# A spectral filter and a state-space layer behind one gate: order of the first loads, folds three row groups ahead, and GpSimd in written order

## The chip, the cores and the metric

The kernel runs on one core of a Trainium2 chip. A core has TensorE (PE in the profile; its weight loads are PEld), VectorE (DVE), ScalarE (ACT), GpSimd (POOL) and SyncE (SP), each with its own instruction queue, and DMA engines that they share. The metric is device time in microseconds: 359.55 us is the median of three runs before the change (358.8, 359.55, 362.57). Inputs and the output are bf16.

## The reference

x has 2048 tokens of 1024 features. Two branches read it, and a gate per token mixes them:

```
g = sigmoid(sum(x * gate_w, over features))
a = irfft2(rfft2(x) * (w_r + i w_i))            # over tokens and features
Lam = Lambda_re + i Lambda_im;  Lam_bar = exp(exp(log_dt) * Lam)
Bu = x @ (((Lam_bar - 1) / Lam) * (B_re + i B_im)).T
h_t = Lam_bar * h_(t-1) + Bu_t                  # a scan over the 2048 tokens
b = 2 * Re(h @ (C_re + i C_im).T) + x * Dskip
out = g * a + (1 - g) * b
```

## The kernel before

**Tokens.** Row group j (0 to 15) is the 128 tokens that are j modulo 16. `load_x(j)` brings it transposed into `xQ[:, :, j, :]` (L194, a transposing DMA of 256 KB from SP).

**The spectral front** is one pass over the 16 row groups. `fold(j)` (L645 to L650) adds and subtracts the two halves of the features on DVE and leaves `preT`. `fd(j)` (L330) multiplies by the constant G on PE (eight matmuls, L334), and ACT copies the product to X1 (L337). `s1(j)` (L340) is the first step of the transform over tokens (four matmuls with the constant T2, L346); A1 is copied out by ACT or, for row groups 6, 8, 10, 12, 14 and 15, by DVE (L349). GpSimd issues its store to DRAM (L350, 256 KB). A1 lies in the tiles `CT`, eight row groups in each half; the transposes of C into the same tiles (`load_C`, L547) come later, when the stores have read them. `keep_A1` (L353) keeps one column of A1.

`front()` (L739) issues for its row group j: the fold of j + 2, `fd(j + 1)`, `s1(j)`, and then some pieces of the tables.

**The tables** (`make_tab`, L207) are the rotations of the state-space scan: four tables of two blocks. Each goes through DVE (angles, L212, L774, L776), ACT (L778 Abs, L779 sine, L781 cosine, L223, L228), DVE (L229, L234), and GpSimd: it spreads `rz` (L214, L215) and casts sine and cosine to bf16 (L219, L225). The buffers of sine and cosine are single, so the sine of one table waits for the casts of the table before. A table is a generator of four pieces; `front` runs one piece in row groups 4 to 7, and two in each from 8 on.

A group of small DVE operations (L786 to L815), which waits for the sine and cosine of a few angles on ACT, stands in DVE's order between row groups 2 and 3.

**The state-space branch.** `unit(c, q)` projects 256 tokens by half of B (64 matmuls, L298; two copies by ACT, L300), and DVE turns, scans (L273) and turns back. The first unit begins in row groups 14 and 15. `early` multiplies by C (L562). These are woven with the later spectral steps until 300 us; then come the last tiles and the output.

**The gate** (`gate`, L673) is 32 matmuls; then GpSimd stores z to DRAM (L681) and loads it back in another order as `zt` (L683).

**W's columns** (`load_Wcols`, L709): two GpSimd copies give `Wp` and `Wf` a value everywhere (they read row group 12 of xQ, L710 and L711), ten GpSimd DMAs fetch two columns of w_r and w_i (L716 to L720, small packets), and three GpSimd copies make `Wc` (L722 to L724). PE reads it at L382, DVE at L389.

**What sets the order.** PE, DVE and ACT run in the order in which the program is written (`manual_schedule`, L167). For GpSimd and SP a planner chooses the order when the program is built. In the profile GpSimd spread all of `rz` first (16 to 22 us), issued three stores of A1 (22 to 26), waited for row group 12 of x (36.5), and went through W's columns, with two stores among them, to 51.9; casts and stores followed.

SP issued x, T2 and B in the order of L661 to L665: the list gives the row groups behind each of which one load of B follows (5, 7, 9 and 11 to 15). G's two loads were issued by ACT at the very start (L174), ahead of five small vectors (L177).

Of the kernel before, what the change touches and what calls it, by code (L numbers as in the profile page):

```python
# [14 lines left out]
BF16 = mybir.dt.bfloat16  # L15
# [8 lines left out]
P = 128  # L24
# [85 lines left out]
def kernel(  # L110
# [17 lines left out]
    nc = tc.nc  # L128
# [4 lines left out]
    cG = nc.inline_tensor(hc["G"], name="c_G").ap()  # L133
# [30 lines left out]
    gta = ictx.enter_context(tc.tile_pool(name="gta", bufs=2, side="right"))  # L164
    psA = ctx.enter_context(tc.tile_pool(name="psA", bufs=2, space=PSUM, reuse_waits="tile"))
    psU = ctx.enter_context(tc.tile_pool(name="psU", bufs=2, space=PSUM, reuse_waits="tile"))
    guard = tc.manual_schedule(engines={mybir.EngineType.PE, mybir.EngineType.DVE, mybir.EngineType.Activation})  # L167
    guard.__enter__()


    fft = {}
    fft["G"] = pre.tile([P, 2, 4, K], BF16, name="G_sb")
    for cls in range(2):
        nc.scalar.dma_start(out=fft["G"][:, cls], in_=cG[:, cls])  # L174
    vec8 = tmp.tile([8, 5, P], BF16, name="vec8")
    for i, src in enumerate((B_Lambda_re, B_Lambda_im, B_log_dt, B_Dskip, gate_w)):
        nc.scalar.dma_start(out=vec8[:, i, :], in_=src.rearrange("(j p) -> j p", p=P))  # L177
# [15 lines left out]
    def load_x(j):  # L193
        nc.sync.dma_start_transpose(out=xQ[:, :, j, :], in_=x_v[j])  # L194

    def load_T2(a, b):
        nc.sync.dma_start(out=fft["T2"][:, a:b], in_=cT2[:, a:b])
# [3 lines left out]
    def load_B(n):  # L201
        for _ in range(n):
            jb, ri = next(parts_B)
            nc.sync.dma_start_transpose(out=BT[jb][:, ri], in_=(B_B_re, B_B_im)[ri][P * jb:P * (jb + 1), :])  # L204


    def make_tab(jp):  # L207
        sh = [P, 2, TC]
        js = slice(2 * jp, 2 * jp + 2)
        ang = tmp.tile(sh, FP32, name="ang")  # L210
        for j in range(2):
            nc.vector.tensor_scalar_mul(out=ang[:, j], in0=tau_f, scalar1=thp[:, 2 * jp + j:2 * jp + j + 1])  # L212
            jb = 2 * jp + j
            nc.gpsimd.tensor_copy(out=rz[:, jb, :], in_=r_sb[:, jb:jb + 1].to_broadcast([P, TC]))  # L214
            nc.gpsimd.memset(rz[:, jb, 0:1], 0.0)  # L215
        sn_f = tmp.tile(sh, FP32, name="sn_f")
        cs_f = tmp.tile(sh, FP32, name="cs_f")
        yield from sincos(tmp, ang, sh, sn_f, cs_f, "rot")
        nc.gpsimd.tensor_copy(out=tab[:, 1, js, :], in_=sn_f)  # L219
        t1 = tmp.tile(sh, FP32, name="t1")  # L220
        t2 = tmp.tile(sh, FP32, name="t2")
        for j in range(2):
            nc.scalar.activation(out=t1[:, j], in_=sn_f[:, j], func=ACT.Copy, scale=ci[:, 2 * jp + j:2 * jp + j + 1])  # L223
        yield
        nc.gpsimd.tensor_copy(out=tab[:, 0, js, :], in_=cs_f)  # L225
        for j in range(2):
            jb = 2 * jp + j
            nc.scalar.activation(out=t2[:, j], in_=cs_f[:, j], func=ACT.Copy, scale=ci[:, jb:jb + 1])  # L228
            nc.vector.scalar_tensor_tensor(out=tab[:, 2, jb, :], in0=cs_f[:, j], scalar=cr[:, jb:jb + 1], in1=t1[:, j],  # L229
                                           op0=ALU.mult, op1=ALU.subtract)  # L230
        yield
        for j in range(2):
            jb = 2 * jp + j
            nc.vector.scalar_tensor_tensor(out=tab[:, 3, jb, :], in0=sn_f[:, j], scalar=cr[:, jb:jb + 1], in1=t2[:, j],  # L234
                                           op0=ALU.mult, op1=ALU.add)
# [73 lines left out]
    def vector(us):  # L309
        owed[0] += us  # L310
        while work and owed[0] > 0:
            cost, piece = work.pop(0)
            piece()
            owed[0] -= cost
        if not work:
            owed[0] = min(owed[0], 0.0)
# [221 lines left out]
    def step():  # L538
        v = next(gen, None)
        while v in ("ia", "ib"):  # L540
            (after_ia if v == "ia" else after_ib)()
            v = next(gen, None)
        return v
# [99 lines left out]
    preTs = {}  # L643

    def fold(j):  # L645
        preTs[j] = gta.tile([P, 8, P], BF16, name="preT", bufs=3)
        to = preTs[j].rearrange("p d (g q) -> p d g q", g=2)
        lo, hi = (xQ[:, 4 * i:4 * (i + 1), j, :].rearrange("p d (q g) -> p d g q", g=2) for i in range(2))
        nc.vector.tensor_add(out=to[:, 0:4], in0=lo, in1=hi)  # L649
        nc.vector.tensor_sub(out=to[:, 4:8], in0=lo, in1=hi)  # L650
# [4 lines left out]
    def keep_warm(n):  # L655
        psw = psA.tile([P, 2, K], FP32, name="psw", tag="ps")
        for i in range(n):
            nc.tensor.matmul(psw[:, i % 2, :], lhsT=idle[:, 0:P], rhs=idle, start=True, stop=True)

    keep_warm(8)  # L660
    for j, b in enumerate((0, 0, 0, 0, 0, 1, 0, 1, 0, 1, 0, 1, 1, 1, 1, 1)):  # L661
        load_x(j)
        if j in (1, 2, 6):
            load_T2(*{1: (0, 2), 2: (2, 8), 6: (8, 16)}[j])
        load_B(b)  # L665
    assert step() == "front"
    fold(0)
    fft["fd"](0)
    fold(1)
    zsb = tmp.tile([P, K], FP32, name="zsb")  # L670
    zt = cpool.tile([P, 16], FP32, name="zt")

    def gate():  # L673
        zps = psA.tile([P, K], FP32, name="zps_g", tag="ps")
        for d8 in range(8):
            for i in range(4):
                nc.tensor.matmul(zps[32 * i:32 * (i + 1), :], lhsT=gw32[:, d8, :], rhs=xQ[:, d8, 4 * i:4 * (i + 1), :],
                                 start=(d8 == 0), stop=(d8 == 7), tile_position=(0, 32 * i))
        nc.scalar.copy(out=zsb.rearrange("p (m j) -> p m j", j=4), in_=zps.rearrange("p (j m) -> p m j", j=4))
        with nc.allow_non_contiguous_dma(reason="gate by token tiles"):  # L680
            nc.gpsimd.dma_start(out=z_dram.rearrange("(n i j) -> i n j", i=4, j=4),  # L681
                                in_=zsb[0:P:32, :].rearrange("i (n j) -> i n j", j=4))
            nc.gpsimd.dma_start(out=zt, in_=z_dram.rearrange("(t p) -> p t", p=P))  # L683
# [25 lines left out]
    def load_Wcols():  # L709
        nc.gpsimd.tensor_copy(out=Wp.rearrange("p r b c -> p (r b c)"), in_=xQ[:, 0, 12, 0:64])  # L710
        nc.gpsimd.tensor_copy(out=Wf, in_=xQ[:, 0, 12, 0:2])  # L711
        with nc.allow_non_contiguous_dma(reason="two columns of W"):
            for ri, W in enumerate((A_w_r, A_w_i)):
                fl = W.rearrange("s k -> (s k)")[K:K + (S - 1) * (K + 1)].rearrange("(s k) -> s k", k=K + 1)
                at = lambda b: bass.AP(W.tensor, W.offset + K + (K + 1) * b, [[16 * (K + 1), P], [K + 1, 15], [1, 2]])
                nc.gpsimd.dma_start(out=Wp[:, ri, 0:15], in_=at(0))  # L716
                nc.gpsimd.dma_start(out=Wp[0:P - 16, ri, 15], in_=fl[15:16 * (P - 16):16, 0:2])
                nc.gpsimd.dma_start(out=Wp[P - 16:P - 1, ri, 15], in_=fl[16 * (P - 16) + 15:S - 1:16, 0:2])
                nc.gpsimd.dma_start(out=Wp[P - 1:P, ri, 15:16, 0:1], in_=W[S - 1:S, K:K + 1].unsqueeze(0))
                nc.gpsimd.dma_start(out=Wf[:, ri:ri + 1], in_=W.rearrange("(p b) k -> p b k", b=16)[:, 0, 0:1])  # L720
        Wc = fft["Wc"].rearrange("p b (c r) -> p r b c", r=2)
        nc.gpsimd.tensor_copy(out=Wc[:, :, :, 1], in_=Wp[:, :, :, 0])  # L722
        nc.gpsimd.tensor_copy(out=Wc[:, :, 1:16, 0], in_=Wp[:, :, 0:15, 1])
        nc.gpsimd.tensor_copy(out=Wc[:, :, 0, 0], in_=Wf)  # L724

    def chain(*items):
        for item in items:
            yield from item

    def halves(gen, n):  # L730
        for _ in range(n):
            next(gen, None)
# [4 lines left out]
    tables = iter(())  # L737

    def front(pieces=0):  # L739
        j = at[0]  # L740
        at[0] += 1
        if j + 2 < 16:
            fold(j + 2)
        if j + 1 < 16:
            fft["fd"](j + 1)
        fft["s1"](j)
        for _ in range(pieces):
            next(tables, None)
# [41 lines left out]
    for _ in sincos(sp, ang2, [P, 2, 8], s2c, c2c, "a2"):  # L790
        front()
# [25 lines left out]
    tables = chain(*(make_tab(jp) for jp in range(4)))  # L817
    while at[0] < 16:
        j = at[0]
        front(0 if j < 4 else 1 if j < 8 else 2)  # L820
        if j == 8:
            fft["keep_A1"](0)
        if j == 12:
            load_Wcols()
        if j >= 14:
            halves(ssm, 1)
            vector(2.0)
    gate()
    fft["keep_A1"](1)
    load_small()  # L830
    load_B(8)
    for _ in tables:
        pass
    tctx.close()
    for q in range(8):
        load_C(q)
# [95 lines left out]
```

## Time and profile before

| what | us |
|---|---|
| median of the runs | 359.55 |
| the profiled execution | 363.51 |
| its span, first to last instruction | 361.7 |
| PE busy | 328.7 (91%) |
| DVE busy | 295.2 (82%) |
| ACT busy | 156.8 (43%) |
| GpSimd busy | 45.8 (13%) |

| stretch, us | what runs in it | PE busy | DVE busy | ACT busy | DMA share | GB/s |
|---|---|---|---|---|---|---|
| 0 to 10 | first loads | 3.57 | 0.33 | 0.00 | 0.94 | 156 |
| 10 to 24 | row groups 0 to 3 | 12.83 | 9.00 | 9.07 | 1.03 | 222 |
| 24 to 48 | row groups 4 to 9 | 18.13 | 18.21 | 14.21 | 1.20 | 179 |
| 48 to 58 | row groups 9 to 11 | 1.35 | 2.03 | 5.52 | 1.17 | 265 |
| 58 to 77 | the last row groups, three tables | 14.22 | 13.18 | 10.58 | 1.07 | 228 |
| 77 to 87 | first unit, gate | 10.00 | 4.94 | 3.85 | 0.95 | 231 |
| 87 to 151 | units, first outputs | 62.32 | 61.94 | 16.52 | 0.55 | 108 |
| 151 to 300 | units, outputs, spectral steps | 148.13 | 136.07 | 76.93 | 0.65 | 170 |
| 300 to 361.7 | last tiles | 58.14 | 49.49 | 20.10 | 0.77 | 133 |

How to read it: the slices of the page divide the span in 40, each digit the busy share in tenths; PEclk is the granted clock of TensorE in the same way. The chain of waits goes back from the last instruction to what released it. The timeline gives start, duration, engine, line, operation, output and inputs, and in brackets the idle time before it with what ended it. Waits are inferred from semaphores, so the name in a bracket can be the wrong one of several. A DMA share can read above 1 in a short stretch.

### The profile page before, as it was taken

The page shows a single profiled execution, that of the slowest core. Times are in us where ns is not written, and L with a number is a line of the kernel's source. Part 1 is how long each engine was busy: PE and PEld are TensorE (multiplying, and loading weights), DVE is VectorE, ACT ScalarE, POOL GpSimd, SP SyncE. Part 2 cuts the span into 40 slices and gives each one's busy share as a digit, 9 for nine tenths or more (in the row PEclk, how much of TensorE's full clock was granted, in tenths as well). Part 3 has the DMA queues.
Part 4 walks back from the last instruction along what each step waited for, and adds up shares of the span by engine and source line. Part 5 has one row for each costly group of instructions (what it writes and reads, how often), then busy time and mean ns, then how long its engine had stood idle before and what let it go on. Part 6 is the DMA issues. An engine that isn't in the chain of part 4 may idle for free.

```text
span 361.7 us, 5961 instructions
## 1 busy us (share of the span) xinstructions
PE 328.7 (91%) x2314; PEld 205.1 (57%) x2314; DVE 295.2 (82%) x443; ACT 156.8 (43%) x200; POOL 45.8 (13%) x80
## 2 busy tenths in 40 slices
PE   3778826599999998999999999999999999999996
PEld 1222211147898647465666657577975786555652
DVE  0567818656999999999999999999995499999961
ACT  0494725572332312365565656245663334344410
POOL 1270853222100000000000000000000001212220
PEclk9698985879999999999999999999999999999999
DMA  9999999996999123178899996297622106975794
GB/s 158 214 201 227 169 197 295 197 193 204 121 197 208 26 87 90 43 201 177 231 291 247 284 241 178 80 248 195 175 63 87 58 2 104 136 139 119 115 134 159
DMA packets 96252, 58.69 MB, mean 162 GB/s; under 512 B 71096, under 2 KB 86976, under 8 KB 96096
## 3 DMA queue, kind: packets, MB, share of 16 engines
q1 hardware_dynamic: 91408, 50.40, 62.0%
q0 software_dynamic: 4448, 6.86, 11.9%
q10 hardware_dynamic: 368, 1.06, 1.2%
q8 instruction: 18, 0.29, 0.4%
q14 instruction: 10, 0.08, 0.1%
HBM read 26.30 MB, written 17.83 MB: 122 GB/s over the span
## 4 chain that ended last, share of the span: by engine, by line
PE 60%; DVE 21%; SPq 8%; DMA 5%; ACT 2%; issue 2%; POOL 1%; DVEq 0%; ACTq 0%; POOLq 0%
PE ps_y L562 22%; PE psu L298 19%; DVE h L273 6%; SPq L194 6%; PE ps_h L562 4%; PE ps_id L593 3%; SPq L204 2%; PE ps_is L501 2%; PE ps_is L476 2%; PE ps_is L477 2%; DMA Wp<-in_A_w_r_dram 2%; PE ps_s L452 2%; DVE su L260 2%; DVE h L261 2%; DMA Wp<-in_A_w_i_dram 2%
## 5 line engine op out<-in xcount | busy, mean ns | idle before, releaser
L298 PE MATMUL psu<-xQ,BT 128*128 128x256 bf16 x1024 | 115.2, 273 | 0.8 <-ACT ye L580 0.5
L298 PEld LDWEIGHTS <-BT 128*128 128x128 bf16 x1024 | 99.4, 98 | 15.5 <-issue 2.4
L562 PE MATMUL ps_y<-CT,h 128*128 128x512 bf16 x448 | 101.3, 379 | 0.0
L562 PEld LDWEIGHTS <-h 128*128 128x128 bf16 x512 | 49.6, 98 | 55.2
L273 DVE TENSOR_TENSOR_SCAN h<-rz,h 128x1024 bf16<-128x1024 f32 x32 | 72.0, 2280 | 0.4
L300 ACT CAST h<-psu 128x1024 bf16<-128x1024 f32 x32 | 32.4, 1012 | 70.5 <-PE psu L298 70.5
L334 PE MATMUL ps_fd<-G_sb,preT 128*128 128x512 bf16 x128 | 37.4, 445 | 19.7 <-DVE preT L649 13.5
L608 POOL DMA_DIRECT2D BT<-y_scratch x10 | 11.9, 1187 | 240.7 <-DVE BT L602 236.5
L334 PEld LDWEIGHTS <-preT 128*128 128x128 bf16 x128 | 12.6, 109 | 43.3 <-DVE preT L649 25.5
L580 ACT ACTIVATE ye<-ps_y,omg 128x512 f32<-128x512 f32 x20 | 12.7, 684 | 35.1 <-PE ps_y L566 30.6
L260 DVE TENSOR_TENSOR su<-h,tab 128x2048 bf16<-128x2048 bf16 x16 | 19.6, 1223 | 4.3 <-ACT h L300 3.5
L454 ACT CAST X<-ps_s 128x1024 bf16<-128x1024 f32 x16 | 16.2, 1014 | 10.9 <-PE ps_s L452 10.9
L261 DVE TENSOR_TENSOR h<-h,tab 128x2048 bf16<-128x2048 bf16 x16 | 19.6, 1225 | 0.8
L285 DVE TENSOR_TENSOR h<-h,tab 128x2048 bf16<-128x2048 bf16 x16 | 19.6, 1225 | 0.5
L337 ACT CAST X<-ps_fd 128x1024 bf16<-128x1024 f32 x16 | 16.1, 1006 | 8.1 <-PE ps_fd L334 8.1
L284 DVE TENSOR_TENSOR sg<-h,tab 128x2048 bf16<-128x2048 bf16 x16 | 19.5, 1219 | 0.0
L649 DVE TENSOR_TENSOR preT<-xQ 128x512 bf16<-128x512 bf16 x16 | 11.1, 695 | 9.0 <-DMA xQ<-in_A_x_dram 9.0
L479 ACT CAST C<-ps_is 128x1024 bf16<-128x1024 f32 x16 | 16.1, 1007 | 3.5 <-issue 3.5
L503 ACT CAST ZT<-ps_is 128x1024 bf16<-128x1024 f32 x16 | 15.5, 1021 | 4.3 <-PE ps_is L501 4.3
L229 DVE SCALAR_TENSOR_TENSOR tab<-cs_f,cr,t 128x256 bf16<-128x256 f32 x8 | 4.8, 642 | 14.7 <-ACT t L223 14.7
L346 PE MATMUL ps_s<-X,raw 64*128 64x512 bf16 x64 | 11.1, 428 | 5.7 <-ACT X L337 5.7
L593 PE MATMUL ps_id<-raw,ZT 128*128 128x256 bf16 x128 | 15.9, 273 | 0.0
(182 smaller groups left out, 364.9 us busy)
## 6 DMA issues: line engine op xcount, KB each, us to landing
y_scratch<-ye SPq DMA_DIRECT2D x20, 256.0 KB, 3.5
turn_scratch<-CT POOLq DMA_DIRECT2D x16, 256.0 KB, 4.7
Bb<-turn_scratch SPq DMA_DIRECT2D x16, 256.0 KB, 4.6
turn_scratch<-C SPq DMA_DIRECT2D x16, 256.0 KB, 5.4
raw<-turn_scratch SPq DMA_DIRECT2D x16, 256.0 KB, 4.3
Wb<-in_A_w_r_dram SPq DMA_DIRECT2D x32, 127.8 KB, 4.0
Wb<-in_A_w_i_dram SPq DMA_DIRECT2D x32, 127.8 KB, 4.1
out_dram<-BT SPq DMA_DIRECT2D x14, 256.0 KB, 3.2
```

What stands on the lines that cost most here:

```text
L194: nc.sync.dma_start_transpose(out=xQ[:, :, j, :], in_=x_v[j])
L260: nc.vector.tensor_mul(out=su, in0=u[:, ::-1], in1=bc(1))
L261: nc.vector.tensor_mul(out=u, in0=u, in1=bc(0))
L273: nc.vector.tensor_tensor_scan(out=seg, data0=rz[:, js].rearrange("p j t -> p (j t)"), data1=seg, initial=0.0, op0=ALU.mult, op1=ALU.add)
L284: nc.vector.tensor_mul(out=sg, in0=u[:, ::-1], in1=bc(3))
L285: nc.vector.tensor_mul(out=u, in0=u, in1=bc(2))
L298: nc.tensor.matmul(psu[:, j, :], lhsT=BT[4 * q + j][:, ri, d8, :], rhs=xQ[:, d8, :, 16 * c:16 * (c + 1)], start=(d8 == 0), stop=(d8 == 7))
L300: nc.scalar.copy(out=u[:, ri].rearrange("p b (m j) -> p b m j", j=16), in_=psu.rearrange("p b (j m) -> p b m j", j=16))
L334: nc.tensor.matmul(ps[:, cls, :], lhsT=preTs[j][:, 4 * cls + d4, :], rhs=G_sb[:, cls, d4, :], start=(d4 == 0), stop=(d4 == 3))
L454: nc.scalar.copy(out=X2, in_=ps2)
L562: nc.tensor.matmul(psy, lhsT=hs[c, jb // 4][:, ri, jb % 4, P * tq:P * (tq + 1)], rhs=CT[ri][:, jb, 512 * dh:512 * (dh + 1)], start=(i == 0 ...
L593: nc.tensor.matmul(pse[:, slot, :], lhsT=ZT_t[:, i, tb, :], rhs=fft["Gi"][:, i, :], start=(kb == 0), stop=(kb == 1))
```

## The change

Five edits. G's loads move from ACT's queue to SP's, behind row group 0 of x. No load of B stands among the first eight row groups; one follows each of row groups 8 to 15. Folds run three row groups ahead, with a fourth `preT` buffer. GpSimd runs in written order: a store of A1 stands behind its row group, and the table's spreads and casts where the pieces stand. `load_Wcols` moves from behind row group 12 to behind the gate, the last copy of A1's column and the small constants; the second eight loads of B, and the call that drains the tables, move ahead of the gate.

```diff
-    guard = tc.manual_schedule(engines={mybir.EngineType.PE, mybir.EngineType.DVE, mybir.EngineType.Activation})
+    guard = tc.manual_schedule(engines={mybir.EngineType.PE, mybir.EngineType.DVE, mybir.EngineType.Activation, mybir.EngineType.Pool})
...
     fft["G"] = pre.tile([P, 2, 4, K], BF16, name="G_sb")
-    for cls in range(2):
-        nc.scalar.dma_start(out=fft["G"][:, cls], in_=cG[:, cls])
...
-        preTs[j] = gta.tile([P, 8, P], BF16, name="preT", bufs=3)
+        preTs[j] = gta.tile([P, 8, P], BF16, name="preT", bufs=4)
...
-    for j, b in enumerate((0, 0, 0, 0, 0, 1, 0, 1, 0, 1, 0, 1, 1, 1, 1, 1)):
+    for j in range(16):
         load_x(j)
+        if j == 0:
+            for cls in range(2):
+                nc.sync.dma_start(out=fft["G"][:, cls], in_=cG[:, cls])
         if j in (1, 2, 6):
             load_T2(*{1: (0, 2), 2: (2, 8), 6: (8, 16)}[j])
-        load_B(b)
+        if j >= 8:
+            load_B(1)
     assert step() == "front"
     fold(0)
     fft["fd"](0)
     fold(1)
+    fold(2)
...
-        if j + 2 < 16:
-            fold(j + 2)
+        if j + 3 < 16:
+            fold(j + 3)
...
         if j == 8:
             fft["keep_A1"](0)
-        if j == 12:
-            load_Wcols()
         if j >= 14:
             halves(ssm, 1)
             vector(2.0)
+    for _ in tables:
+        pass
+    load_B(8)
     gate()
     fft["keep_A1"](1)
     load_small()
-    load_B(8)
-    for _ in tables:
-        pass
+    load_Wcols()
     tctx.close()
```

## The prediction

> **What bounds the kernel now.** I read the busy slices first, then the chain of waits, then each engine in order of time. The slices (9 us each) split the run in two: TensorE (PE) has holes in the first eight and is full from the ninth on.
>
> ```profile
> PE   3778826599999998999999999999999999999996
> PEclk9698985879999999999999999999999999999999
> ```
>
> Asked by stretches, PE is busy 50.1 us of the first 77, and 148.1 of the 149 from 151 to 300. So the end moves by what the spectral front (16 row groups, up to 77 us) gains or loses, unless something later is tied to another clock. The chain of waits, cut to the front, shows what holds it (start, us, what):
>
> ```profile
> 31.45 5.00 DMA xQ<-in_A_x_dram
> 36.51 0.23 POOL Wp L710
> ...
> 37.59 6.83 DMA Wp<-in_A_w_r_dram
> 44.42 0.28 issue
> 44.70 5.59 DMA Wp<-in_A_w_i_dram
> ...
> 51.90 0.55 POOL tab L219
> ...
> 53.02 0.99 ACT X L337
> ```
>
> GpSimd (POOL) waits for row group 12 of x, fetches W's columns, waits for them, and only then casts the first table's sine (L219). ScalarE (ACT) wants that buffer for the second table's sine. The same in order of time, with the idle time in brackets:
>
> ```profile
> 10.96 3.59 PE L334 MATMUL ps_fd<-G_sb,preT 128*128 128x512 bf16 x8 [6.17 <-DMA vec<-in_B_Lambda_im_dram]
> 24.01 0.60 PE L346 MATMUL ps_s<-X,raw 64*128 64x512 bf16 x4
> 28.34 3.45 PE L334 MATMUL ps_fd<-G_sb,preT 128*128 128x512 bf16 x8 [3.73 <-DVE preT L649]
> 32.35 1.90 PE L334 MATMUL ps_fd<-G_sb,preT 128*128 128x512 bf16 x8
> 52.48 0.63 ACT L779 ACTIVATE sn_f<-ang 128x512 f32<-128x512 f32 x1 [6.15 <-POOL tab L219]
> 62.28 0.63 ACT L778 ACTIVATE rot_kk<-ang 128x512 f32<-128x512 f32 x1 [4.25 <-DVE ang L776]
> 94.28 1.19 POOL L683 DMA_DIRECT2D zt<-z_scratch  x1 [5.50 <-DMA z_scratch<-zsb]
> 107.61 0.17 PE L382 MATMUL Wrev_ps<-Wc,JP_sb 128*128 128x4 bf16 x1
> ```
>
> Three holes: the start (first fold at 10.21), the wait for fold(5) (3.73, after which eight matmuls take 3.45 instead of 1.90, at a low granted clock), and the 6.15 on ACT. From 57 on the front is paced by a ring without GpSimd or the lookahead: fold, A1 copy, L234, angles on VectorE (DVE), then Abs, Sin, X, A1, Cos, t1 on ACT, then L229 on DVE: 10.3 us per table, two row groups (L229 at 55.97, 66.29, 76.53). The change leaves that ring as it is.
>
> **The change part by part** (times are those of the profiled execution; fd, s1, X, A1 are the steps of `front`).
>
> *G behind x0.* x0 was issued at 0.74 and landed 9.4 later, beside G's 1.05 MB on ACT's queue; the median x load lands in 4.3. Now x0 is alone, fold(0) at about 5 to 6, and fd(0) waits for G. x0 and G are 1.31 MB. At 156 GB/s (first 10 us, start-up included) that is 8.4; at 222 (10 to 24 us), with data flowing from 1.5, it is 7.4. fd(0) stays at the low clock: 8 + 3.6 + 0.6 for L752 gives fd(1) at 12.2 against 15.07. But the small DVE operations that follow stand behind fold(2) now, so behind x2: 1.94 MB, 10.2 to 12.4, plus 1.2 for the fold: vecT at about 12.8 against 15.17. I take **2.3 gained**, of 0 (the same bytes must pass) to 4. G's two issues cost SP 2 x 0.58, which is hidden while the transfers lag the issues (x2's issue took 3.95 for lack of room). ACT's five vec loads no longer wait behind G: they were the last to land before L752 (14.96), now fd(0) is.
>
> *Folds three ahead.* fold(5) now precedes the DVE block that waits for cos (23.04 to 27.60). fd(5) follows s1(3) at 24.6 with no wait. Next late is fold(6), first behind the block: done at 28.8, so fd(6) at 28.9 instead of 32.35, 3.4 earlier; PE idles 2.4 before it, and at the low clock it loses 1.55 of that. **1.8 gained**, of 0 to 3.4. The fourth preT buffer adds no wait. At the other end, fold(15) is no longer what releases the last step. Today fd(15) (73.13, 3.46 long) ends at 76.6 and s1(14) starts at 76.53; then s1(14) needs only X(14), done at 74.56: 1.9 earlier. PE has then idled some 4 us (fd(15) ran a row group ahead), so unit(0,0), 3.67 today, starts at the low clock: eight matmuls went from 1.90 to 3.45 to 3.60 in such places, a loss of about 1.6. **0.3 gained**, of 0 to 1.9.
>
> This is where a rule speaks against the change. The Trainium skill, "TensorE: Matmul & The Clock Gate", section "What's actually happening", puts the halving after an idle window of about 3.4 us. The trace agrees at 3.73 idle, but a gap of 2.90 also gave 3.60 here. By the page, fd(6) would stay at full clock and the sum would be 1.6 better; by the row it doesn't.
>
> *GpSimd in written order.* Stores of A1 stand after each s1, tables' casts after the store of their row group. The first sine cast comes right behind the store of row group 6, and the sine that waited is asked for at 46.3. Nothing of W stands between. The 6.15 goes in full: behind it X(10), A1(9), Cos, t1 are ready to run, as they did at 53.02. Next late is the ring above, which begins at once. **6.15 gained**, of 0 to 6.15. Two costs. The rz copies (8, 0.39 to 0.91 each) move from 16 to 22 us into the later row groups; folds beside them took 0.88 instead of 0.68: **0.4 lost**, of 0 to 1.6. And stores no longer pause from 25.9 to 36.7: four to six more (0.26 MB each) pass among x8 to x12. At 222 GB/s that is 4.7 us for x11, which else lands at 33; B loads among the x loads are the same three. So x11 is there at 33 to 37.7, and fold(11) wants it at about 36 (40.34, where DVE was ready for the next fold, less 4.1): **0.7 lost**, of 0 to 1.7. x12 may be 2 late, but L229 behind it waits for t1 until 45.
>
> "SBUF — State Buffer" of the Trainium skill, section "A bandwidth-pool intuition that's wrong (but worth ruling out)", has a transfer issued by GpSimd go from some 620 ns to 3100 beside a VectorE copy that locks GpSimd out, which speaks against these stores; by it, as an estimate, 2.5 us more for each store so met. The rows show 0.73 per store issue beside DVE work too, and no run here separates it.
>
> *W's columns last.* They now stand behind the gate: z's store (87.65), then zt, which holds GpSimd until z has landed (94.28, issued 95.47). Before, from the first copy (36.51) to the last (51.90) it took 15.4, of which 1.6 to 2.3 are A1 stores in between: 13.1 to 13.8. So Wc is ready at 108.6 to 109.3, on the clock of today, and all of this moves with the front. PE comes to L382 at 107.50: it waits 1.1 to 1.8 there. VectorE, which holds the chain from 86 to 147, comes to Wc at 109.54 and to PE's product at 109.65; it loses 0 to 0.3. PE's own delay fits in what it waits for DVE later (1.24 at L412, 0.44 at L443). **0.3 lost**, of 0 to 2.6. Behind Wcols on GpSimd stand Wb's memsets (95.46, then 109.5); should Wb's loads (104.75) wait for them, SP runs 5 late, and the xs load behind them (115.25) lands by 125, used at 132.8.
>
> *Loads.* B's first eight are used from 77.06, the last of these now issued with x15 at about 45. The second eight were done issuing at 61.7 and are used from 86.6: 15 of cover with any gain so far. JP and KRS move behind eight B loads (14 us), used at 107. CT's second half waits for the last store (88.9) and moves with the front; used 13 us after it has landed. The columns' small packets now share the DMA engines with it: in 36 to 48 the rate was 148 GB/s against 210 before, so about 4 lost of 13.
>
> Sum: 2.3 + 1.8 + 0.3 + 6.15 - 0.4 - 0.7 - 0.3 = 9.1, about **9.0 us**. The profiled execution took 363.51 (span 361.7 and 1.8 around it), 1.1% above the median 359.55; the terms are waits, not shares, so I subtract from the median: **350.5**.
>
> **The rivals.**
>
> *The transfers set the pace.* The DMA share is above 0.9 all through the front, and the bytes are the same. Then the start gives nothing, folds wait for x11 to x13, and only the GpSimd wait counts: 6.15 - 0.4 - 0.3 + some lookahead, 6 gained, **353.5**. Against it: x loads came in 4.3 after issue, and PE never waited for one after the first. 20%.
>
> *It doesn't do what it says.* The ACT wait is replaced by another in the same place (x10's fold, a store that holds GpSimd ahead of the cast). Left are start and lookahead less the losses, 3: **356.5**, on the edge of no change. 11%.
>
> *Slower: W's columns hold PE.* Place: L382. They need two landings in series (6.83, then 5.4 to 8.5), now while CT's eight transposes are issued in one burst of 14.09. If each landing took that burst, Wc would be ready 14 to 15 later, at 124; PE would stand 16.5, DVE 14.4, and the end is 14.4 - 9.0 = 5.4 later: **365**. It turns slower than before once Wc is more than 9 later than reckoned. Against it: the columns met B's transposes last time, with the DMA share as high. 6%.
>
> *Better.* No low clock at fd(6) and unit(0,0), no x wait: 9.0 + 1.5 + 1.6 + 0.7, 12.8 gained, **346.7**. 11%.
>
> **How the numbers follow.** The forecast (348 to 353) has 52%. The range 346.5 to 356.5 takes in the better case, the pace case and half of the third. What a measurement here can tell from no change is about 1%, so 355.95 is the bound: faster are forecast, pace, better and a little of the third, 0.84; within 1%, 0.10; slower, 0.06.
>
> **What would show it.** fd(0) at about 8, with x0's fold near 5; no fd waiting 3.7 at row group 5; no wait of ACT's L779 for L219; table rings still 10.3 apart; unit(0,0) at about 68 and its second half's copy at 77 instead of 85.9; a short PE wait at L382 on GpSimd or a Wp load. The prediction is wrong if the ring itself is longer, if DVE waits for x loads from row group 9 on, if L382 waits over 3 us, or if the stretch from unit(0,0) to the end isn't the same length as now.

## The result

The changed kernel gained less than was forecast: the ratio to the kernel before is 0.9875, with a 95% interval of 0.9834 to 0.9917, some 4.5 us of 362 where the forecast was 9.0. The 20 runs of the changed kernel lie between 354.6 and 367.2 us, those of the kernel before between 358.8 and 363.9 (median 362.1, where the three runs shown before the prediction had 359.55). The ratio counts the runs within 1.5% of the fastest of each kernel, which are eight of the changed kernel's (median 358.1, outside the range of 346.5 to 356.5) and all of the other's. Over all twenty the changed kernel's median is 361.8, so that most of its runs gained next to nothing. The profile below is of a run of 366.0 and shows the loss at its larger size; a short run stands further on.

Line numbers have shifted: in the changed kernel the products with G are L332, the copy of X L335, the sine L782, the casts of the tables L217 and L223, the load of `MT`, a constant of 1.5 MB, L359 (L361 before), z's store L684, zt L686, W's columns L713 to L727, the product of the columns L380 (L382 before) and their copy on VectorE L387 (L389 before).

The busy slices of the changed kernel (364.2 us in 40 slices):

```profile
PE   5989458799629999999999999999999999999996
PEclk9999986999958999999999999999999999999999
```

The front is denser than before. A new hole stands in the eleventh and twelfth slice, where the kernel before had none, and the granted clock falls in and behind it. The timeline of the changed kernel, front first (start, duration, engine, line, operation; the idle time before it in brackets):

```profile
7.65 3.57 PE L332 MATMUL ps_fd<-G_sb,preT 128*128 128x512 bf16 x8 [2.84 <-DMA G_sb<-c_G]
25.54 1.90 PE L332 MATMUL ps_fd<-G_sb,preT 128*128 128x512 bf16 x8 [1.36 <-DVE preT L647]
42.47 0.61 ACT L782 ACTIVATE sn_f<-ang 128x512 f32<-128x512 f32 x1
66.50 3.67 PE L296 MATMUL psu<-xQ,BT 128*128 128x256 bf16 x32
74.34 1.01 ACT L298 CAST h<-psu 128x1024 bf16<-128x1024 f32 x1 [3.13 <-PE psu L296]
...
76.02 0.53 SPq L359 DMA_DIRECT2D raw<-c_MT  x1
76.91 20.98 SPq L545 DMA_TRANSPOSE CT<-in_B_C_im_dram  x8
77.08 1.13 POOL L684 DMA_DIRECT2D z_scratch<-zsb  x1 [3.50 <-ACT zsb L682]
88.81 1.19 POOL L686 DMA_DIRECT2D zt<-z_scratch  x1 [10.60 <-DMA z_scratch<-zsb]
...
106.28 0.25 POOL L725 COPY Wc<-Wp 128x32 bf16<-128x32 bf16 x1 [4.84 <-DMA Wp<-in_A_w_i_dram]
106.79 0.21 DVE L387 CAST Wc_f<-Wc 128x64 f32<-128x64 bf16 x1 [7.69 <-POOL Wb L521]
106.81 0.16 PE L380 MATMUL Wrev_ps<-Wc,JP_sb 128*128 128x4 bf16 x1 [9.60 <-POOL Wb L521]
```

The first hole of the front is shorter, the other two are gone: the first product comes at 7.65 instead of 10.96, with no wait of 3.73 at row group 5, and the second table's sine comes at 42.47 with no wait instead of 52.48. ScalarE's second copy for the first unit, the mark that I use for the end of the front, stands at 74.34 instead of 84.91: 10.6 us gained. Then PE waits 9.60 and VectorE 7.69 for `Wc`, and the lead is spent. Behind the wait the next 128 matmuls take 16.53 instead of 14.13 (low clock after the idle time), and PE waits 1.3 more for `Bb` loads. From the mark to the end it is 289.9 us instead of 276.8.

The chain of waits of the changed kernel says how `Wc` came to be late:

```profile
77.08 11.45 DMA z_scratch<-zsb
...
90.00 0.63 POOL Wp L713
...
92.64 7.42 DMA Wp<-in_A_w_r_dram
100.06 0.28 issue
100.34 5.74 DMA Wp<-in_A_w_i_dram
```

z's store took 11.45 us to land, against 6.3 before; zt stands behind it on GpSimd, and the columns behind zt.

### The profile page after: what moved, and what is told of

It reads as the page before. It is cut to its first block, busy times and chain, and to the rows that moved or that the text cites. A ratio compares the mean times of both kernels' runs of the same rounds, so it can differ in the third digit from the quotient of the medians.

```text
span 364.2 us, 5969 instructions
## 1 busy us (share of the span) xinstructions
PE 329.7 (91%) x2314; PEld 206.5 (57%) x2314; DVE 298.5 (82%) x443; ACT 156.9 (43%) x200; POOL 45.9 (13%) x80
## 3 DMA queue, kind: packets, MB, share of 16 engines
q0 software_dynamic: 4448, 6.86, 11.3%
## 4 chain that ended last, share of the span: by engine, by line
PE 58%; DVE 16%; DMA 12%; ACT 5%; issue 5%; SPq 2%; POOL 1%; POOLq 0%; ACTq 0%; DVEq 0%
PE psu L296 21%; PE ps_y L560 19%; PE ps_h L560 4%; PE ps_id L591 3%; DMA Bb<-turn_scratch 3%; DMA z_scratch<-zsb 3%; PE ps_fd L332 2%; DMA Wp<-in_A_w_r_dram 2%; PE ps_is L499 2%; DMA Wp<-in_A_w_i_dram 2%; PE ps_s L450 2%; DVE preT L648 2%; DMA G_sb<-c_G 1%; PE ps_is L475 1%; PE ps_is L474 1%
## 5 line engine op out<-in xcount | busy, mean ns | idle before, releaser
L296 PE MATMUL psu<-xQ,BT 128*128 128x256 bf16 x1024 | 117.6, 276 | 0.8 <-ACT ye L578 0.5
L296 PEld LDWEIGHTS <-BT 128*128 128x128 bf16 x1024 | 100.7, 99 | 16.6 <-issue 2.0
L332 PE MATMUL ps_fd<-G_sb,preT 128*128 128x512 bf16 x128 | 36.0, 432 | 4.2 <-DMA G_sb<-c_G 2.8
L332 PEld LDWEIGHTS <-preT 128*128 128x128 bf16 x128 | 12.5, 107 | 27.2 <-issue 11.2
L335 ACT CAST X<-ps_fd 128x1024 bf16<-128x1024 f32 x16 | 16.0, 1003 | 10.2 <-PE ps_fd L332 10.2
L348 POOL DMA_DIRECT2D turn_scratch<-CT x16 | 11.8, 738 | 49.0 <-ACT CT L347 30.5
L647 DVE TENSOR_TENSOR preT<-xQ 128x512 bf16<-128x512 bf16 x16 | 11.4, 711 | 7.7 <-DMA xQ<-in_A_x_dram 7.6
```

Of the source, the lines that this page charges most:

```text
L296: nc.tensor.matmul(psu[:, j, :], lhsT=BT[4 * q + j][:, ri, d8, :], rhs=xQ[:, d8, :, 16 * c:16 * (c + 1)], start=(d8 == 0), stop=(d8 == 7))
L332: nc.tensor.matmul(ps[:, cls, :], lhsT=preTs[j][:, 4 * cls + d4, :], rhs=G_sb[:, cls, d4, :], start=(d4 == 0), stop=(d4 == 3))
```

## The experiments

All comparisons are with the kernel before on the same chip and in the same session; versions of different sessions are compared by these ratios. The first four start from the changed kernel, the next four from the version with W's columns ahead of the gate, the first of the two last ones is the changed kernel again, and the last starts from the version with the pieces first.

**W's columns ahead of the gate.**

```diff
     load_B(8)
+    load_Wcols()
     gate()
     fft["keep_A1"](1)
     load_small()
-    load_Wcols()
```

> W's columns ahead of the gate on GpSimd, all else as in the changed kernel. Theory (the loss is the series: z's store, its landing, zt, then the columns): Wc is ready near 88, PE does not wait at the product of W's columns, the first half unit's second copy by ScalarE stays at 74.3, and the end falls by the whole gain of the front, 9 to 11 us under the kernel before (ratio 0.970 to 0.975). Rival (C's transposes stretch every landing of GpSimd's small packets, wherever they stand): Wc near 98, 1 to 2 us of wait, ratio 0.980. Rival (the loss is in the stretch behind, not in this wait): ratio as the changed kernel's, 0.9875.

Measured: 352.7 us (352.4 to 354.3) against 362.2, ratio 0.9745 (0.9699 to 0.979). Its timeline on PE, and on GpSimd:

```profile
97.52 0.17 PE L380 MATMUL Wrev_ps<-Wc,JP_sb 128*128 128x4 bf16 x1
```

```profile
85.90 1.18 POOL L727 COPY Wc<-Wf 128x2 bf16<-128x2 bf16 x1
87.03 1.15 POOL L684 DMA_DIRECT2D z_scratch<-zsb  x1
95.30 1.20 POOL L686 DMA_DIRECT2D zt<-z_scratch  x1 [7.12 <-DMA z_scratch<-zsb]
```

`Wc` is ready at 87, and PE comes to it at 97.52 with no wait in brackets. The mark is at 74.82 and the rest takes 276.6, as before the change (276.8). So the series behind the gate was the loss, and the front's gain passes to the end in full when it is gone. zt comes later than before the move and nothing waits for it.

**The loads ahead of the gate, the joining copies behind zt.** As above, but the three copies into `Wc` stay behind the gate, as a function of their own.

> The ten loads of W's columns ahead of the gate, the three copies that join them behind zt. Theory: the landing of the columns lies beside the landing of z; Wc is ready at about 93 to 94, ahead of the product's turn at 97, ratio 0.970 to 0.975, and the gate's values are earlier than with all of the columns ahead. Rival (stretched landings): Wc at 97 to 100, ratio 0.975 to 0.982.

Measured: 354.4 (353.4 to 358.1), ratio 0.9796 (0.9741 to 0.985). In the profiled run, the slowest (358.1), zt was issued at 98.69 after 8.03 of waiting, the copies came behind it, and PE waited 4.13. The rival holds in part: the columns' own landings were stretched (the last of their issues waited 5.55 for an earlier one) while C's eight transposes, issued from 75.74 on, took 24.98 instead of 14.09.

**The columns behind row group 12 again, GpSimd in written order.**

```diff
             fft["keep_A1"](0)
+        if j == 12:
+            load_Wcols()
...
     load_small()
-    load_Wcols()
```

> The columns where they were in the kernel before, behind row group 12, but GpSimd in written order. Theory: the casts that the second and third table's sine wait for stand ahead of them, so ScalarE's wait of 6 us does not come back; the last table's casts and the stores of row groups 13 to 15 are held some 14 us, C's second half starts near 80 instead of 77, ratio 0.970 to 0.980. Rival (the place behind row group 12 is what cost the 6 us, whatever the order of the casts): ScalarE waits 5 us or more for GpSimd again, ratio 0.985 or more.

Measured: 356.3 (355.1 to 357.0), ratio 0.9825 (0.976 to 0.9889). ScalarE's wait for a cast didn't come back. The last casts and three stores were held until 77 to 83 us, C's second half started at 87.9, and the rest took 278.5. The place was not what cost 6 us before; that the first casts stood behind it was.

**Without C's imaginary half.**

```diff
-        for ri, src in enumerate((B_C_re, B_C_im)):
+        for ri, src in enumerate((B_C_re,)):
```

> The changed kernel without the eight loads of C's imaginary half (left out; the output's second product then uses other data). Theory (z's 11.5 us to landing comes from those eight transposes, issued in one burst with it): z lands in 6 to 7 us, zt is issued near 84 instead of 88.8, PE's wait at the product of W's columns falls from 9.6 to 2 to 5, ratio 0.970 to 0.98. Rival (small packets of the store itself are slow): z still lands in 10 to 12, the wait stays 8 to 10, ratio 0.985 to 0.99.

The eight loads of C's imaginary half are left out. Measured: 356.3 (354.0 to 358.1), ratio 0.9832 (0.977 to 0.9894). The timeline of GpSimd and of PE in it:

```profile
80.88 1.14 POOL L684 DMA_DIRECT2D z_scratch<-zsb  x1 [4.09 <-ACT zsb L682]
87.51 1.19 POOL L686 DMA_DIRECT2D zt<-z_scratch  x1 [5.50 <-DMA z_scratch<-zsb]
```

```profile
101.71 0.16 PE L380 MATMUL Wrev_ps<-Wc,JP_sb 128*128 128x4 bf16 x1 [0.71 <-POOL Wb L521]
```

zt is issued 6.6 us behind z's store, and PE waits 0.71. The wait is gone as the theory had it, further than its 2 to 5. The time fell less than I expected. In the profiled run (358.1) the mark is late, 78.14: the first product began at 8.63, and the first unit met the low clock. The rest took 278.2. The transposes are not all that differs from the long run above: `MT`'s load was issued at 74.53, 6.3 ahead of z's store, where there it was 1.1 ahead.

**Folds two ahead.** The two edits of the fold undone, W's columns ahead of the gate.

> The version with W's columns ahead of the gate (352.7 us), but folds two row groups ahead as before. The prediction gave the lookahead 1.8 at row group 5 and 0.3 at the end: the first unit's second copy by ScalarE comes 1 to 3 us later than with three ahead, and the time is 354 to 355.5. Rival (the hole at row group 5 is hidden by the table ring behind it): no difference, 352.5 to 353.

Measured: 354.9 (353.7 to 355.2) against 360.9, ratio 0.9823 (0.9774 to 0.9872); against 0.9745 with three ahead this is 2.8 us, with intervals that overlap. In the profile the wait of 3.74 at row group 5 is back, and the first unit starts at 68.42 instead of 65.31; half of that is given back, since the unit then runs at the full clock (3.67 instead of 5.33).

**The loads as before.** G on ScalarE's queue first, B's loads among the x loads.

> The version with W's columns ahead of the gate, but G's loads first on ScalarE's queue and B's loads among the x loads as before. The prediction gave the start 2.3 (0 to 4): the first eight matmuls with G start near 11 instead of 7.5, the time is 354.5 to 356. Rival (only the same bytes in another order, made up by the wait for cos): 352.5 to 353.5.

Measured: 356.9 (356.7 to 357.8), ratio 0.9883 (0.9827 to 0.9938): 5.0 us, also the mark is 4.5 later (79.35). The first product starts at 12.57; in the kernel before, with the same loads, it was 10.96, so part of the 5 is how one run's loads fell.

**GpSimd in the planner's order.** `Pool` out of the list of `manual_schedule`, W's columns ahead of the gate in the text.

> The version with W's columns ahead of the gate in the text, but GpSimd in the planner's order, which puts two of the columns' loads and the wait for row group 12 of x ahead of the first table's casts. The prediction gave GpSimd's order 6.15: ScalarE waits 3 to 6 us for the cast of the first sine again, the time is 356 to 359. Rival (the order of the casts doesn't matter once x comes earlier): 352.5 to 354.

Measured: 354.9 (353.4 to 355.6), ratio 0.9823 (0.9772 to 0.9875): 2.8 us, less than expected, again with intervals that overlap. ScalarE's timeline, and then VectorE's:

```profile
41.37 0.63 ACT L782 ACTIVATE sn_f<-ang 128x512 f32<-128x512 f32 x1 [1.99 <-POOL tab L217]
53.82 0.63 ACT L782 ACTIVATE sn_f<-ang 128x512 f32<-128x512 f32 x1 [2.57 <-POOL tab L217]
```

```profile
44.87 0.88 DVE L227 SCALAR_TENSOR_TENSOR tab<-cs_f,cr,t 128x256 bf16<-128x256 f32 x2 [4.45 <-ACT t L221]
57.31 1.29 DVE L227 SCALAR_TENSOR_TENSOR tab<-cs_f,cr,t 128x256 bf16<-128x256 f32 x2 [5.52 <-ACT t L221]
67.55 1.29 DVE L227 SCALAR_TENSOR_TENSOR tab<-cs_f,cr,t 128x256 bf16<-128x256 f32 x2 [4.04 <-ACT t L221]
```

The waits for casts are back, 4.56 together, and the two sine rows are the place that the prediction named. But L227 takes 0.88 and 1.29 here, and 1.63 in the changed kernel, and the last two of these rows are 10.24 apart instead of 10.96. So written order takes away about 4.6 of waiting and pays part of it back in slower VectorE operations.

**The tables' pieces ahead of the row group.**

```diff
         at[0] += 1
+        for _ in range(pieces):
+            next(tables, None)
         if j + 3 < 16:
             fold(j + 3)
         if j + 1 < 16:
             fft["fd"](j + 1)
         fft["s1"](j)
-        for _ in range(pieces):
-            next(tables, None)
```

> The version with W's columns ahead of the gate, with the pieces of the tables ahead of the row group's fold, products and copies instead of behind them. Theory (from row group 9 the front is paced by the ring over VectorE and ScalarE, 10.3 us per table before and 10.96 in the changed kernel): the folds, the copies of A1 and one copy of X leave the ring, it falls to 7 to 8 us per table, and two to three rings give 6 to 9 us: 344 to 347. Rival (transfers of x or the copies bound the row groups as well): 350 to 352.5.

Measured: 347.5 (347.2 to 347.9) against 360.9, ratio 0.9625 (0.958 to 0.9671): another 4.3 us under the columns ahead of the gate, by the ratios. The ring on VectorE, in the changed kernel and then in this one:

```profile
45.95 1.63 DVE L227 SCALAR_TENSOR_TENSOR tab<-cs_f,cr,t 128x256 bf16<-128x256 f32 x2 [2.76 <-ACT t L221]
56.91 1.63 DVE L227 SCALAR_TENSOR_TENSOR tab<-cs_f,cr,t 128x256 bf16<-128x256 f32 x2 [2.84 <-ACT t L221]
67.87 1.63 DVE L227 SCALAR_TENSOR_TENSOR tab<-cs_f,cr,t 128x256 bf16<-128x256 f32 x2 [4.04 <-ACT t L221]
```

```profile
40.86 1.42 DVE L227 SCALAR_TENSOR_TENSOR tab<-cs_f,cr,t 128x256 bf16<-128x256 f32 x2 [0.48 <-ACT t L221]
50.02 1.23 DVE L227 SCALAR_TENSOR_TENSOR tab<-cs_f,cr,t 128x256 bf16<-128x256 f32 x2 [0.80 <-ACT t L221]
59.06 1.23 DVE L227 SCALAR_TENSOR_TENSOR tab<-cs_f,cr,t 128x256 bf16<-128x256 f32 x2 [0.80 <-ACT t L221]
```

A table takes 9.1 instead of 10.96, not 7 to 8, and the mark is at 69.55. The ring did pace the front; what holds it at 9.1 was not taken apart.

**The changed kernel again.** No edit.

> The changed kernel unaltered, for a second profile, since its 20 runs lie between 354.6 and 367.2. Theory (the spread is PE's wait at the product of W's columns, which follows the landing of z and of the columns): the front to the first unit's second copy by ScalarE stays within 73 to 78 us, the stretch from there to the end is 276.7 plus 1 to 1.5 times that wait, and the wait is less than 9.6 in a shorter run: a run of 358 goes with a wait of about 4. Rival (the spread lies elsewhere): the wait is again 9 to 10 with another time.

Measured: 354.6, 361.9, 363.9 and 365.6; the profile is of the first. GpSimd, the DMA issues of SyncE, and PE in it:

```profile
76.95 1.14 POOL L684 DMA_DIRECT2D z_scratch<-zsb  x1 [3.49 <-ACT zsb L682]
83.05 1.19 POOL L686 DMA_DIRECT2D zt<-z_scratch  x1 [4.96 <-DMA z_scratch<-zsb]
```

```profile
72.99 0.53 SPq L359 DMA_DIRECT2D raw<-c_MT  x1
...
79.25 13.81 SPq L545 DMA_TRANSPOSE CT<-in_B_C_im_dram  x8
```

```profile
99.36 0.16 PE L380 MATMUL Wrev_ps<-Wc,JP_sb 128*128 128x4 bf16 x1 [2.29 <-POOL Wb L521]
```

The mark is at 74.20, as in the other profile (74.34), and the rest takes 278.6 instead of 289.9. The shorter time goes with the shorter wait, as the theory had it, though the rest is only 1.9 longer than the 276.7 without a wait, 0.8 times the wait. The two runs differ by 11.4 us, and 11.3 of them lie behind the mark. In the long run C's transposes start 0.17 ahead of z's store, in the short one 2.3 behind it. The transposes need the tile that the last store of A1 reads. In the short run that store, issued at 72.73 with `MT`'s load right behind it, took 6.4 us to land, and the transposes waited for it. In the long run it was issued at 72.86 and had landed after 3.3; the transposes came when SyncE, later with C's first half, had issued an x load (74.39) and `MT`'s load (76.02) ahead of them. So `MT`'s 1.5 MB, z's store and the transposes went out within 1.1 us of one another there. Two profiles don't show that every run of the spread has this cause; the version with the columns ahead of the gate spreads over 1.9 us in six runs, the changed kernel over 12.5 in its twenty.

**The spreads of rz ahead of the first store.** The loop over `rz` taken out of `make_tab` and put ahead of `sincos`, pieces first.

> The version with the pieces of the tables first (347.5 us), with all eight spreads of rz on GpSimd ahead of the first store instead of in the tables. Theory (GpSimd's work beside VectorE lengthens VectorE's operations in the ring): L777 goes from 0.58 back to 0.43 and the two angle multiplications from 0.88 to 0.62, the ring from 9.1 to 8.7, and two to three rings give about 1 us: 346 to 347. Rival (it was not GpSimd): no change, 347.3 to 348; or the first store, 2 us later, delays something: slower.

Measured: 347.3 (346.7 to 348.1), ratio 0.9615 (0.9575 to 0.9655) against 0.9625: no difference that this measurement can tell. VectorE's operations did get shorter: L777 (L778 there) takes 0.43 to 0.47, after 0.43 to 0.74, and the ring falls from 9.1 to 8.66. The mark came at 68.41 instead of 69.55.

What z's store met, in all twelve profiles (us):

| version | z's store issued | C's transposes issued | `MT`'s load issued | store to zt's issue |
|---|---|---|---|---|
| columns at row group 12 | 82.91 | 87.90 to 99.0 | 77.93 | 6.0 |
| changed, short run | 76.95 | 79.25 to 93.1 | 72.99 | 6.1 |
| before | 87.65 | 88.90 to 103.0 | 81.30 | 6.6 |
| no imaginary half of C | 80.88 | none | 74.53 | 6.6 |
| GpSimd in the planner's order | 78.20 | 80.54 to 98.0 | 79.66 | 9.3 |
| loads as before | 91.56 | 84.68 to 96.5 | 75.75 | 6.1 |
| folds two ahead | 89.20 | 83.26 to 95.4 | 73.22 | 7.3 |
| pieces first | 83.20 | 75.49 to 92.8 | 74.60 | 7.3 |
| columns ahead of the gate | 87.03 | 81.67 to 94.6 | 72.76 | 8.3 |
| columns split | 89.50 | 75.74 to 100.7 | 73.47 | 9.2 |
| pieces first, rz early | 80.62 | 77.99 to 95.1 | 77.10 | 9.7 |
| changed, long run | 77.08 | 76.91 to 97.9 | 76.02 | 11.7 |

The store took 6.0 to 6.6 in four of the five profiles in which it was issued ahead of the transposes or without them, and 6.1 to 11.7 in the seven in which it was issued among them. Which of the two is issued first does not settle it: in the planner's order the store went 2.3 ahead and still took 9.3. In the three profiles with 9.3, 9.7 and 11.7 the transposes began 0.9 us behind `MT`'s load, and the store was issued within 3.6 us of both. `MT`'s load alone is not it either: in the short run the store followed it by 4.0 and took 6.1. No run moved `MT`'s load by itself, so how much of the 11.7 it makes stays open.

## Why the prediction was wrong

**What failed is one step: "W's columns last", 0.3 lost, of 0 to 2.6.** It took z's landing from the row of the kernel before (87.65 to 94.28) and let it move with the front. In that row the transposes of C's second half began 1.25 us behind z's store. They wait for the last store of A1 and for SyncE, z waits for the gate, and all move, but not as a block: in the long run the transposes went 0.17 ahead of the store, and `MT`'s load, which is in no term of the prediction, 1.1 ahead. z then landed in 11.45; zt, held until then, came 5.1 later than the reckoning; GpSimd needed 1.9 more before the first of the columns' issues; and two landings in series followed. PE waited 9.60 where I had 1.1 to 1.8, VectorE 7.69 where I had 0 to 0.3. In the short run, where z went first, PE waited 2.29 and VectorE 0.38 for `Wc`, close to the step's numbers, and the run took 354.6.

**The slower rival had the place and the cause**, landings stretched by C's burst in front of L382, at 6%. It stretched the columns' two landings (6.83 to 14.09 each). Those took 7.42 and 5.74; the stretched one was z's, which I had treated as done. Its 16.5 on PE and 14.4 on VectorE came to 9.60 and 7.69 in the long run. Its weight was too low because the argument against it ("the columns met B's transposes last time") was about the wrong transfer.

**The range was too narrow for the same reason.** z's landing took 5.8 in one profile of the changed kernel and 11.45 in the other, by what was in flight beside it; I gave it one value. The base was low as well: 359.55 was the median of three runs and 362.1 that of twenty, so 2.5 of the 7.6 between 350.5 and 358.1 are not the change's. That the short run lies 9.0 under the profiled execution before (354.55 and 363.51), the very sum of the forecast, is partly luck: the front gained 10.7 for the 9.45 of its terms, and 1.8 went behind it for 0.3.

The other steps, point by point:

- *What bounds the kernel* held. With no wait at `Wc`, the stretch behind the mark is 276.6 to 277.5 in the six profiles with the columns ahead of the gate, against 276.8 before, wherever the mark stood (68.4 to 79.4).
- *G behind x0*, 2.3: the first product came at 7.65 for a forecast of about 8, x0's fold at 4.53 for 5 to 6. Undone, it costs 5.0 by the ratios, part of it scatter; the term was too small.
- *Folds three ahead*, 1.8 and 0.3: 2.8 by the ratios. fd(6) started at 25.54, 6.8 earlier than before, where start and this term together had promised 4.1. It ran at the full clock after 1.36 idle, where I had charged 1.55 for the low one.
- *GpSimd in written order*, 6.15: the sine of the second table came 10.0 earlier, for 10.25 promised by the three terms up to there. So the wait went in full. But the cost beside it was mis-sized: I had 0.4 for slower VectorE operations, from folds beside rz. In the changed kernel the ring is 10.96 per table instead of 10.28, 1.36 over two rings, and L227 beside GpSimd's casts (1.63, where the kernel before had 1.29 to 1.37) is a part of it. I had written that the change leaves the ring as it is. The Trainium skill, "SBUF — State Buffer", section "Who interferes with whom", says that a VectorE instruction with two SBUF inputs contends with a GpSimd instruction that reads SBUF; these rows agree.
- *x11 late*, 0.7: no fold waited for x after row group 1. The loads kept ahead.
- *Wb's memsets behind the columns*: they did hold Wb's loads, which started at 106.82 as soon as the first memset was done (106.69), and the planner put the xs load ahead of them. PE's 1.3 of waiting for `Bb` loads further on was not counted either; what delayed those was not taken apart.

**The clock rule.** I weighed a rule of the Trainium skill ("TensorE: Matmul & The Clock Gate", section "What's actually happening": half clock after an idle window of about 3.4 us) against the row of the kernel before where 2.90 idle also gave 3.60, and followed the row. The first unit's 32 matmuls sort much as the rule has it, with the step a little above its figure: after 3.35, 3.39, 3.50 and 3.52 of idle time ahead of the step before them they took 3.67, after 3.63 and 4.15 they took 5.33, after 4.50 they took 5.84; one profile between (3.78) has 4.67. The row that misled me (57.99) had a gap of 5.75 three microseconds ahead of it, with 1.04 of work between: the granted clock was 0.50 from 54.0 to 62.6, so it had not come back yet. Another row of the same profile with 2.90 of idle time (68.23) took 2.40, and I passed over it.

## What to carry to other kernels

When a step moves behind a wait on another transfer, ask which transfers may be in flight with that one after the move; a landing time read from one profile holds for the traffic that it met there. Put small loads that a later product needs ahead of a store and reload on the same in-order queue, not behind it: the same edit with the columns ahead of the gate gave a ratio of 0.9745 instead of 0.9875. And when holes of an engine are closed, look for the ring of dependencies that paces what is left: here two lines moved, pieces ahead of the row group, gave 4.3 us on top of the columns ahead of the gate, about as much as the whole change had (347.5 us, 0.9625).

## What the runs showed of the hardware that was not expected

- A store of 8 KB in small packets, followed to the next issue that waits for it, took 6.0 to 6.6 us in the four profiles named above and up to 11.7 beside eight transposing loads of 256 KB (the table).
- The eight transposes took 11.1 to 14.1 us to issue in the six profiles in which the 1.5 MB load of `MT` was issued 6 us or more ahead of them, 17.1 to 21.0 in the four in which it was 0.9 ahead, and 25.0 in the one with 2.3, where the loads of W's columns were in flight too. Those small loads alone did not do it: in the short run the transposes took 13.81 beside them. That `MT`'s load is the cause is not shown.
- GpSimd's casts lengthen VectorE operations that run beside them by more than the 0.2 I had read from the folds: a pair of L227 took 1.63 beside both casts of a table, 0.88 beside none.
